# Expert weight loads and splits placed by the program on ACT, POOL and DVE

## The chip, the core and the metric

The kernel runs on one core of one Trainium2 chip. The metric is the device time of one launch in microseconds, the median of several runs. Five engines work side by side, each through its own instruction list in order: TensorE (PE: matmuls, with PEld for the loading of their stationary operands), VectorE (DVE), ScalarE (ACT), GpSimd (POOL), and SyncE (SP), which here only issues DMA transfers.

## What is computed

Sparse causal attention, then a dense layer pair, then eight experts that each take exactly 288 of 2304 tokens.

```python
attn_out = _attn_ref(q, k, v)                # 4 x 8 heads, 576 tokens, 64 wide; two masks
x = attn_out.transpose(0, 2, 1, 3).reshape(2304, 512)
h = x @ w_in                                 # 512 -> 2048
x = np.maximum(0.01 * h, h) @ w_out          # 2048 -> 512
logits = x @ w_gate                          # 8 experts
# pairs (token, expert) in falling order of logit; a token goes to the first expert
# in this order that has room left (288 places each) -> assigned
for e in range(8):
    mask = assigned == e
    h = np.maximum(x[mask] @ w1[e], 0.0)     # 512 -> 1024
    out[mask] = h @ w2[e]                    # 1024 -> 512
```

## The kernel before

**Numbers in two halves.** Every large matrix product is made of three: each fp32 operand is split into a high part in the matmul's own format and the rest, and high x high, high x low and low x high are added up. For a weight tile the high part is a copy on ACT (`hi`, `whi`) and the low part a subtraction on POOL or DVE (`lo`, `wlo`), which must wait for that copy.

**Dense layers.** Tokens go in six blocks of 384. Blocks 0 to 2 pass both layers at once. For blocks 3 to 5 the first layer is run with its results kept (`gd`) or sent to DRAM (`g3d`), and the second layer follows as `second(4)`, `second(5)`, `second(3)`: each has 16 steps `f`, and a step splits one row of `WO` (`split`: `hi` on ACT, `lo` on POOL, two buffers each) and runs nine matmuls of 512 columns (L944 to L946: `hi`, `lo`, `hi` again with the low half of the activations). The last step copies the block out and stores it in `x2d`, from which `gather` later takes an expert's rows.

**Routing.** The greedy assignment is a search on DVE and PE (`search`, `route`, `tokens`, all through one helper at L683): for each of eight rounds k, five threshold counts. A count is: DVE compares (`G`, about 1.4 us for a tile), PE sums (`cnt`, 18 small matmuls), DVE makes a `flag`, PE sums it to `tot`. After the fifth comes a chain of some dozen small DVE operations to the expert's number `ei` and to a pair `tot`, PE makes prefix sums (`po`, L775), DVE makes places, PE gathers them (`pi`, L813), and DVE writes the row numbers `idx`. `pace` takes so many steps of this per step of the dense layer or of an expert, so that the search of later rounds runs under the matmuls of `second` and of the first experts.

**Experts.** `expert(k)` has 32 steps of six matmuls. 16 make `h` (`g3`, L878 to L880; after each two steps ACT writes `hh` and DVE `hl`), 16 make the output (`g4`, L901 to L903), which is turned back (`back`, ACT copies it to `o`) and scattered to DRAM by three indirect DMAs that POOL issues (`put`, L917). The turning of the last quarter and the scatter are put off to the second pair of steps of the next expert. `gather(k + 1)` runs in the last ten steps: POOL issues three indirect DMAs (`xg`, L851), PE turns the rows (`pet`), ACT and DVE split them (`exh`, `exl`).

**Expert weights.** `weights(k)` is a generator over eight pieces of 512 KB, n = 0 to 3 of `w1` and 4 to 7 of `w2`. For each it issues the load on SP into one of three `raw` buffers, copies `whi` on ACT, and subtracts `wlo`: on DVE for n = 1, 5 and 7, on POOL for the rest. `wx` for expert 0 is stepped four times in `second(3)` and finished after `gather(0)`; for expert k + 1 it is made at step 3 of expert k (`values_load` reads the expert's number into SP) and stepped at the even steps from 6 on. The `w2` halves have five buffers, in a pool (`POOLB`) that can only be opened when `second(3)` has ended.

**What sets the order.** The program text gives each instruction a priority and its dependencies; a scheduler then puts each engine's list together and may move an instruction forward as soon as its own model of time has its inputs ready. The search goes through `Soon`, which raises its priority by 2000.

Of the kernel before, what the change touches and what calls it, by code (L numbers as in the profile page):

```python
# [7 lines left out]
F32 = mybir.dt.float32  # L8
F32R = mybir.dt.float32r
# [3 lines left out]
AF = mybir.ActivationFunctionType  # L13
# [5 lines left out]
DM, FF = 512, 2048  # L19
# [7 lines left out]
def body(ctx, tc, q, k, v, w_in, w_out, w_gate, w1, w2, out):  # L27
    nc = tc.nc
# [7 lines left out]
    xa = ctx.enter_context(tc.tile_pool(name="xa", bufs=1, reuse_waits="tile"))  # L36
# [260 lines left out]
    WI = [xa.tile([128, 2, 512], F32, name="WI", tag=f"WI{f}") for f in range(8)]  # L297
    WI = [WI[f // 2][:, f % 2] for f in range(16)]
# [288 lines left out]
    for n in range(64, 96):  # L587
        blk, f = divmod(n, 16)
# [11 lines left out]
        if f % 4 == 0:  # L600
            x = "hl"[f // 4 % 2]
# [53 lines left out]
    m, kh, e1, rem, s, sel, oh = (state(n) for n in (18, 18, 18, 18, 18, 18, 8))  # L655
# [29 lines left out]

    soon = Soon()

    def search():

        soon.tensor_reduce(m, L, axis=AX.X, op=OP.max)  # L690
# [131 lines left out]
    def ind(ap):  # L822
        return bass.IndirectOffsetOnAxis(ap=ap, axis=0)

    def weights(k):
        e = nc.values_load(EXP[k][0:1, 0:1], engines=[mybir.EngineType.SP], min_val=0, max_val=7)
        W[k] = []
        for n in range(8):
            raw = POOLA[0].tile([128, 1024], F32, name="raw", tag="raw", bufs=3)
            if n < 4:  # L830
                nc.sync.dma_start(raw, w1[bass.ds(e, 1), 128 * n:128 * n + 128, :].rearrange("e p m -> (e p) m"))
            else:
                nc.sync.dma_start(raw.rearrange("p (j m) -> p j m", j=2),
                                  w2[bass.ds(e, 1), 256 * (n - 4):256 * (n - 4) + 256, :].rearrange(
                                      "e (j p) m -> p (e j) m", j=2))
            if n < 4 and k % 2:
                hi, lo = (xa.tile([128, 1024], F32R, name="w" + x, tag=f"WI{n + y}") for x, y in (("hi", 0), ("lo", 4)))
            else:
                pool, tag, bufs = (POOLB[0], "w2", 5) if n >= 4 else (POOLA[0], "w1", 4)
                hi = pool.tile([128, 1024], F32R, name="whi", tag=tag + "h", bufs=bufs)  # L840
                lo = pool.tile([128, 1024], F32R, name="wlo", tag=tag + "l", bufs=bufs)
            nc.scalar.activation(hi, raw, AF.Copy)  # L842
            (nc.vector if n in (1, 5, 7) else nc.gpsimd).tensor_sub(lo, raw, hi.bitcast(F32))  # L843
            W[k].append((hi, lo))
            yield

    def gather(k):
        xg = xa.tile([96, 3, DM], F32, name="xg", tag=("xh2", "xl2")[k % 2])
# [20 lines left out]
    def expert(k):  # L869
# [4 lines left out]
        for j in range(8):  # L874
# [9 lines left out]
                left_.pop()()  # L884
            nc.scalar.activation(hh[:, j], p, AF.Relu)  # L885
            nc.vector.scalar_tensor_tensor(hl[:, j], p, 0.0, hh[:, j].bitcast(F32), op0=OP.max, op1=OP.subtract)  # L886
        o = e2.tile([96, 3, DM], F32, name="o", tag="o", bufs=2)

        def back(c, ot):
            pt = bank([96, 3, 128], "pot", "m")  # L890
# [71 lines left out]
    def need(k):  # L962
        while ROUTED[0] <= k:
            next(R, None)
# [16 lines left out]
        if f > 2 and f % 2:  # L981
            fetch(f // 2)
    need(0)
    wx = weights(0)
    for f, _ in enumerate(second(3)):
        pace(0.87)
        if f < 8:
            fetch(f + 8)
        if f % 4 == 1:
            next(wx)  # L990
    right.close()
    POOLB[0] = ctx.enter_context(tc.tile_pool(name="pbx", bufs=1, reuse_waits="tile", side="right"))
    for _ in gather(0):
        pass
    for _ in wx:
        pass
    for k in range(8):
        nxt = iter(())
        for n, _ in enumerate(expert(k)):
            pace(0.45)  # L1000
            if n == 3 and k < 7:
                need(k + 1)
                wx = weights(k + 1)
            if n >= 6 and n % 2 == 0:
                next(wx, None)
            if n == 22 and k < 7:
                nxt = gather(k + 1)
                next(nxt)
            if n >= 22:
                next(nxt, None)  # L1010
        for x in (wx, nxt):
            for _ in x:
                pass


# [28 lines left out]
```

## Time and profile before

| | us |
|---|---|
| median of 3 runs (911.5 to 913.36) | 913.01 |
| the profiled execution, its own time | 920.74 |
| its span, first to last instruction | 919.0 |
| PE busy in it | 860.8 |
| DVE busy | 567.6 |
| POOL busy | 473.1 |
| ACT busy | 442.7 |

The profile follows one execution; times in it are counted from its first instruction. A matmul's end is modelled, and matmuls overlap, so the distance from start to start tells more than the busy time. PEclk is TensorE's granted clock as a share of 2.4 GHz; 0.5 is its other level, 1.2 GHz. The dense layers' last three blocks run from 505 to 634 us, the experts from 643 to 906.

### The profile page before, as it was taken

How to read it: one execution, taken by the hardware profiler on the slowest of the kernel's cores; microseconds unless marked ns; L12 is line 12 of the kernel's file. 1: busy time of each engine (PE TensorE's matmuls, PEld its weight loads, DVE VectorE, ACT ScalarE, POOL GpSimd, SP SyncE). 2: the span in 40 equal slices, each digit the busy share in tenths (PEclk: the TensorE clock that was granted, in tenths of full speed). 3: DMA queues.
4: the chain of work that ended last, by engine and by line, in shares of the span. 5: the costliest groups of instructions: out<-in, count | busy, mean ns of one | idle time of the engine just before them, and what ended most of it. 6: DMA issues, size and time to landing. Idle time of an engine off the chain costs nothing.

```text
span 919.0 us, 17020 instructions
## 1 busy us (share of the span) xinstructions
PE 860.8 (94%) x6272; PEld 723.8 (79%) x6272; DVE 567.6 (62%) x1537; ACT 442.7 (48%) x1098; POOL 473.1 (51%) x394
## 2 busy tenths in 40 slices
PE   8789999799999999999999998996998899999994
PEld 5667766677777777788988776775998899899994
DVE  5778798865546455566545463455677888784330
ACT  4787757464545445544554232222453443535531
POOL 2645655564555465554554455554643625736621
PEclk8899999999999999999999997998999999999998
DMA  7487555420112000142000033342644534626700
GB/s 178 121 191 171 136 147 143 130 61 14 37 35 78 14 14 1 52 157 102 1 1 18 1 104 128 118 139 72 201 153 130 190 114 143 192 96 210 209 27 26
DMA packets 95411, 93.18 MB, mean 101 GB/s; under 512 B 66144, under 2 KB 74336, under 8 KB 95328
## 3 DMA queue, kind: packets, MB, share of 16 engines
q1 hardware_dynamic: 87648, 65.88, 25.2%
q0 software_dynamic: 7680, 26.22, 9.3%
q8 instruction: 49, 0.80, 0.4%
q14 instruction: 34, 0.28, 0.1%
HBM read 76.35 MB, written 15.73 MB: 100 GB/s over the span
## 4 chain that ended last, share of the span: by engine, by line
PE 66%; DVE 9%; DMA 7%; issue 6%; POOL 5%; ACT 4%; SPq 1%; POOLq 0%; ACTq 0%; DVEq 0%
PE p L421 4%; PE q L944 4%; PE p L423 4%; PE p L374 3%; PE p L422 3%; PE q L945 3%; PE q L946 3%; PE p L398 3%; PE g L901 3%; PE g L902 3%; DMA raw<-in_moe_w_dram 3%; PE g L903 3%; PE p L376 3%; PE p L375 3%; PE p L400 3%
## 5 line engine op out<-in xcount | busy, mean ns | idle before, releaser
L353 POOL TENSOR_TENSOR lo<-WI,hi 128x512 fp32r<-128x512 f32 x96 | 127.3, 1326 | 99.2 <-DVE hi L352 58.2
L353 POOL TENSOR_TENSOR lo<-WO,hi 128x512 fp32r<-128x512 f32 x96 | 124.9, 1302 | 97.4 <-ACT hi L350 97.3
L843 POOL TENSOR_TENSOR wlo<-raw,whi 128x1024 fp32r<-128x1024 f32 x40 | 98.1, 2465 | 71.5 <-ACT whi L842 66.7
L350 ACT ACTIVATE hi<-WO 128x512 fp32r<-128x512 f32 x96 | 60.5, 630 | 109.4 <-PE q L946 66.5
L842 ACT ACTIVATE whi<-raw 128x1024 fp32r<-128x1024 f32 x64 | 65.9, 1055 | 45.1 <-DMA raw<-in_moe_w_dram 42.3
L374 PE MATMUL p<-xh,hi 128*128 128x384 f32 x192 | 75.6, 394 | 5.4 <-DVE g L383 5.4
L878 PE MATMUL g<-exh,whi 128*128 128x288 f32 x256 | 79.4, 311 | 0.2 <-DVE hl L886 0.2
L901 PE MATMUL g<-hh,whi 128*128 128x288 f32 x256 | 78.8, 308 | 0.6 <-ACT hh L885 0.6
L879 PE MATMUL g<-exl,whi 128*128 128x288 f32 x256 | 78.1, 306 | 0.0
L880 PE MATMUL g<-exh,wlo 128*128 128x288 f32 x256 | 77.6, 303 | 0.0
L902 PE MATMUL g<-hl,whi 128*128 128x288 f32 x256 | 76.3, 298 | 0.1
L903 PE MATMUL g<-hh,wlo 128*128 128x288 f32 x256 | 76.0, 297 | 0.0
L160 ACT ACTIVATE sc<-sc,mx 96x128 f32<-96x128 f32 (+2 forms) x176 | 67.6, 387 | 16.1 <-DVE mx L158 16.1
L376 PE MATMUL p<-xh,lo 128*128 128x384 f32 x192 | 66.0, 344 | 1.5 <-POOL lo L353 1.5
L421 PE MATMUL p<-xh,hi 128*128 128x384 f32 x192 | 66.4, 346 | 0.0
L375 PE MATMUL p<-xl,hi 128*128 128x384 f32 x192 | 65.8, 342 | 0.6 <-DVE xl L235 0.6
L423 PE MATMUL p<-xh,lo 128*128 128x384 f32 x192 | 64.7, 337 | 0.7 <-POOL lo L353 0.7
L398 PE MATMUL p<-hi,gh 128*128 128x512 f32 x144 | 64.1, 445 | 0.7 <-ACT gh L384 0.7
L422 PE MATMUL p<-xl,hi 128*128 128x384 f32 x192 | 64.4, 335 | 0.0
L182 POOL TENSOR_TENSOR sc<-sc,mx 96x384 f32<-96x384 f32 (+2 forms) x64 | 51.5, 822 | 21.3 <-DVE mx L180 14.0
L400 PE MATMUL p<-hi,gl 128*128 128x512 f32 x144 | 56.9, 395 | 0.0
L843 DVE TENSOR_TENSOR wlo<-raw,whi 128x1024 fp32r<-128x1024 f32 x24 | 47.4, 1976 | 15.1 <-ACT whi L842 15.0
(209 smaller groups left out, 2313.0 us busy)
## 6 DMA issues: line engine op xcount, KB each, us to landing
raw<-in_moe_w_dram SPq DMA_DIRECT2D x64, 512.0 KB
wraw<-in_moe_w_in_dram POOLq DMA_DIRECT2D x16, 512.0 KB, 4.6
wraw<-in_moe_w_out_dram POOLq DMA_DIRECT2D x16, 512.0 KB, 3.9
g<-g3d SPq DMA_DIRECT2D x16, 384.0 KB
rawq<-in_q_dram SPq DMA_DIRECT2D x32, 144.0 KB
rawk<-in_k_dram SPq DMA_DIRECT2D x32, 144.0 KB
x2d<-x SPq DMA_DIRECT2D x18, 256.0 KB
g3d<-gh SPq DMA_DIRECT2D x16, 192.0 KB
```

The source lines that it names most:

```text
L353: nc.gpsimd.tensor_sub(lo, src, hi.bitcast(F32))
L374: nc.tensor.matmul(p1, wh[:, cs], xh[:, c], start=(c == 0), stop=False)
L375: nc.tensor.matmul(p1, wh[:, cs], xl[:, c], start=False, stop=False)
L376: nc.tensor.matmul(p1, wl[:, cs], xh[:, c], start=False, stop=(c == 3))
L398: nc.tensor.matmul(p2[t], gh[:, s], oh, start=(f == 0), stop=False)
L421: nc.tensor.matmul(p1, wh[:, cs], xh[:, c], start=(c == 0), stop=False)
L422: nc.tensor.matmul(p1, wh[:, cs], xl[:, c], start=False, stop=False)
L423: nc.tensor.matmul(p1, wl[:, cs], xh[:, c], start=False, stop=(c == 3))
L843: (nc.vector if n in (1, 5, 7) else nc.gpsimd).tensor_sub(lo, raw, hi.bitcast(F32))
L901: nc.tensor.matmul(p, wh, hh[:, j], start=(j == 0), stop=False)
L902: nc.tensor.matmul(p, wh, hl[:, j], start=False, stop=False)
L903: nc.tensor.matmul(p, wl, hh[:, j], start=False, stop=(j == 7))
```

## The change

`weights` is split into `load(k, n)`, which issues one transfer, and `halves(k, n)`, which makes `whi` and `wlo` of it. Both operations of `halves` are passed to `pin`, which orders each behind the instruction that the program text has just ahead of it on the same engine; what comes later in the text may still be moved ahead of it. There are four `raw` buffers. Of the eight subtractions n = 5 and 7 stay on DVE, n = 1 goes to POOL. The output tile `o` has one buffer in place of two. Expert 0's first four loads are issued ahead of `second(3)`, whose steps 3, 6, 9 and 12 make their halves and issue the next loads; the table `CH` gives the steps of an expert (1, 4, 7 for its own pieces 5 to 7, then 10, 14, 18, 22, 26 for pieces 0 to 4 of the next) and at each of them the next expert's next load.

```diff
+    def pin(x):
+        tc.keep_in_program_order(x[0] if isinstance(x, tuple) else x)
...
-    def weights(k):
-        e = nc.values_load(EXP[k][0:1, 0:1], engines=[mybir.EngineType.SP], min_val=0, max_val=7)
-        W[k] = []
-        for n in range(8):
-            raw = POOLA[0].tile([128, 1024], F32, name="raw", tag="raw", bufs=3)
...
-            nc.scalar.activation(hi, raw, AF.Copy)
-            (nc.vector if n in (1, 5, 7) else nc.gpsimd).tensor_sub(lo, raw, hi.bitcast(F32))
-            W[k].append((hi, lo))
-            yield
+    def load(k, n):
+
+        if n == 0:
+            W[k] = []
+            REG[k % 2] = nc.values_load(EXP[k][0:1, 0:1], engines=[mybir.EngineType.SP], min_val=0, max_val=7)
+        e = REG[k % 2]
+        raw = POOLA[0].tile([128, 1024], F32, name="raw", tag="raw", bufs=4)
...
+        RAWE[k, n] = raw
...
+    def halves(k, n):
+        raw = RAWE.pop((k, n))
...
+        pin(nc.scalar.activation(hi, raw, AF.Copy))
+        pin((nc.vector if n in (5, 7) else nc.gpsimd).tensor_sub(lo, raw, hi.bitcast(F32)))
+        W[k].append((hi, lo))
...
-        o = e2.tile([96, 3, DM], F32, name="o", tag="o", bufs=2)
+        o = e2.tile([96, 3, DM], F32, name="o", tag="o")
...
-    wx = weights(0)
+    for n in range(4):
+        load(0, n)
     for f, _ in enumerate(second(3)):
         pace(0.87)
         if f < 8:
             fetch(f + 8)
-        if f % 4 == 1:
-            next(wx)
+        if f in (3, 6, 9, 12):
+            halves(0, f // 3 - 1)
+            if f < 12:
+                load(0, 3 + f // 3)
...
-    for _ in wx:
-        pass
+    halves(0, 4)
+    load(0, 7)
+    CH = {n: i for i, n in enumerate((1, 4, 7, 10, 14, 18, 22, 26))}
     for k in range(8):
         nxt = iter(())
         for n, _ in enumerate(expert(k)):
             pace(0.45)
-            if n == 3 and k < 7:
-                need(k + 1)
-                wx = weights(k + 1)
-            if n >= 6 and n % 2 == 0:
-                next(wx, None)
+            if n in CH:
+                c = CH[n]
+                if c < 3:
+                    halves(k, 5 + c)
+                elif k < 7:
+                    halves(k + 1, c - 3)
+                if k < 7:
+                    need(k + 1)
+                    load(k + 1, c)
```

The list of POOL from the start of `second(4)` to the first expert, before (lines L353 are `lo` of `WO`, L843 `wlo`, L851 the gathers' DMAs):

```order
L353 TENSOR_TENSOR lo<-WO,hi 128x512 x17
L843 TENSOR_TENSOR wlo<-raw,whi 128x1024
L353 TENSOR_TENSOR lo<-WO,hi 128x512 x3
L843 TENSOR_TENSOR wlo<-raw,whi 128x1024 x2
L353 TENSOR_TENSOR lo<-WO,hi 128x512 x26
L851 DMA xg<-x2d,idx 96x512 x6
```

and in the changed kernel (L855 is `wlo`, L862 the gathers):

```order
L353 TENSOR_TENSOR lo<-WO,hi 128x512 x34
L855 TENSOR_TENSOR wlo<-raw,whi 128x1024
L353 TENSOR_TENSOR lo<-WO,hi 128x512 x3
L855 TENSOR_TENSOR wlo<-raw,whi 128x1024
L353 TENSOR_TENSOR lo<-WO,hi 128x512 x3
L855 TENSOR_TENSOR wlo<-raw,whi 128x1024
L353 TENSOR_TENSOR lo<-WO,hi 128x512 x3
L855 TENSOR_TENSOR wlo<-raw,whi 128x1024
L353 TENSOR_TENSOR lo<-WO,hi 128x512 x3
L862 DMA xg<-x2d,idx 96x512 x6
```

Three `wlo` stood in `second(5)`, two of them in a row; now four stand singly in `second(3)`, from its fourth `lo` on.

The list of DVE in expert 1, where the fifth count of a search round ends, before (L886 is `hl`, L683 the search, `flag` the fifth count's):

```order
L683 TENSOR_SCALAR flag,f_7732<-cnt 64x8
L886 SCALAR_TENSOR_TENSOR hl<-g_7706,hh 128x288
L683 TENSOR_REDUCE n<-tot 128x1
L683 TENSOR_SCALAR o_7753<-tot,n 128x8
L683 TENSOR_TENSOR st<-o_7753,st 128x8
L683 TENSOR_REDUCE e_7756<-st 128x1
L843 TENSOR_TENSOR wlo<-raw,whi 128x1024
L683 TENSOR_SCALAR st<-st,e_7756 128x8
```

and in the changed kernel, from the end of the same chain (L897 is `hl`, the CAST writes the `tot` that PE's `po` reads, `s` is the first to read `po`):

```order
L897 SCALAR_TENSOR_TENSOR hl<-g_7797,hh 128x288
L683 CAST ei<-ev 128x1
L683 SCALAR_TENSOR_TENSOR st<-st,ab 128x36
L683 CAST tot<-st 128x2
L855 TENSOR_TENSOR wlo<-raw,whi 128x1024
L683 SCALAR_TENSOR_TENSOR s_7822<-st,po,ab 128x18
L897 SCALAR_TENSOR_TENSOR hl<-g_7812,hh 128x288
```

The subtraction left the middle of the chain and stands behind the `tot` that PE waits for, but ahead of the last three `hl`.

The list of DVE in expert 3 of the changed kernel, from the third count to the fifth:

```order
L683 SCALAR_TENSOR_TENSOR G<-th_5738,zero_5748,st 128x1152
L855 TENSOR_TENSOR wlo<-raw,whi 128x1024
L683 TENSOR_SCALAR flag,f_8786<-cnt 64x8
L897 SCALAR_TENSOR_TENSOR hl<-g_8723,hh 128x288
L683 SCALAR_TENSOR_TENSOR G<-th_5734,tot,st 128x1152 x2
L897 SCALAR_TENSOR_TENSOR hl<-g_8760,hh 128x288
L897 SCALAR_TENSOR_TENSOR hl<-g_8804,hh 128x288
L683 TENSOR_SCALAR flag,f_8858<-cnt 128x8
L855 TENSOR_TENSOR wlo<-raw,whi 128x1024
L683 SCALAR_TENSOR_TENSOR G<-th_5736,tot,st 128x1152
```

Both subtractions (n = 5, then n = 7) stand inside the search, the second between a `flag` and the next count's `G`.

## Rows read from the trace of the kernel before

**Rows 1.** The page's busy times: us, share of the span, instructions.

```profile
PE 860.8 (94%) x6272; PEld 723.8 (79%) x6272; DVE 567.6 (62%) x1537; ACT 442.7 (48%) x1098; POOL 473.1 (51%) x394
```

**Rows 2.** Windows: second(5), second(3), experts; busy us PE PEld DVE ACT POOL; clock; DMA.

```profile
542.00:592.60 50.60, 45.63 (x263) 34.25 (x263) 23.33 (x53) 16.09 (x24) 28.98 (x20) 0.90 0.42 136
592.60:634.00 41.40, 39.87 (x254) 29.99 (x253) 23.14 (x65) 12.32 (x21) 20.14 (x16) 1.00 0.38 120
...
643.00:906.00 263.00, 253.19 (x2213) 245.16 (x2212) 172.68 (x415) 114.83 (x213) 129.95 (x77) 0.98 0.46 146
```

**Rows 3.** Waits of PE in second(5): for whom, us in total, times, longest.

```profile
PE q L945 <- POOL lo L353: 5.0, 3, 2.9
```

**Rows 4.** Waits of PE in experts 1 to 7 (676 to 906 us).

```profile
PE tot L732 <- DVE flag L683: 3.8, 5, 1.7
PE po L775 <- DVE tot L683: 3.5, 2, 3.4
PE cnt L725 <- DVE G L683: 1.6, 2, 0.8
PE g L901 <- ACT hh L885: 0.6, 1, 0.6
```

**Rows 5.** Timeline of POOL in second(5): start, us, instruction, idle before and its end.

```profile
549.16 2.39 POOL L843 TENSOR_TENSOR wlo<-raw,whi 128x1024 fp32r<-128x1024 f32 x1 [0.95 <-DMA x2d<-x]
558.50 5.70 POOL L843 TENSOR_TENSOR wlo<-raw,whi 128x1024 fp32r<-128x1024 f32 x2
```

**Rows 6.** Timeline of PE: waits in second(5), expert 1 and expert 2.

```profile
552.84 0.61 PE L945 MATMUL q<-lo,g5h 128*128 128x512 f32 x1 [1.80 <-POOL lo L353]
...
692.98 0.16 PE L775 MATMUL po<-tot,tri 128*128 128x2 bf16 x1 [3.36 <-DVE tot L683]
729.30 0.16 PE L732 MATMUL tot<-f,units 64*128 64x1 bf16 x1 [1.74 <-DVE flag L683]
```

**Rows 7.** Windows after the four longest waits; clock is the third number from the end.

```profile
553.00:557.00 4.00, 4.00 (x23) 3.10 (x24) 0.23 (x1) 0.90 (x2) 1.02 (x1) 0.57 0.28 115
566.00:574.00 8.00, 8.00 (x37) 6.08 (x36) 0.17 (x2) 1.13 (x2) 1.94 (x2) 0.57 0.36 131
693.00:697.00 4.00, 4.00 (x20) 4.00 (x20) 2.12 (x9) 1.47 (x2) 2.79 (x2) 0.57 0.81 309
730.00:734.00 4.00, 4.00 (x21) 4.00 (x20) 2.20 (x12) 1.32 (x2) 2.38 (x1) 0.57 0.64 243
```

**Rows 8.** Timeline of POOL in second(3): `lo` of steps 4 and 7.

```profile
601.13 1.29 POOL L353 TENSOR_TENSOR lo<-WO,hi 128x512 fp32r<-128x512 f32 x1 [0.95 <-ACT hi L350]
...
607.50 1.29 POOL L353 TENSOR_TENSOR lo<-WO,hi 128x512 fp32r<-128x512 f32 x1 [0.79 <-ACT hi L350]
```

**Rows 9.** Timeline of PE in second(3): the first matmuls that read those two `lo`.

```profile
602.49 0.49 PE L945 MATMUL q<-lo,g 128*128 128x512 f32 x1
...
609.75 0.39 PE L945 MATMUL q<-lo,g 128*128 128x512 f32 x1
```

**Rows 10.** All uses of tile raw: duration ns min/median/max; then who waited.

```profile
L843 POOL TENSOR_TENSOR wlo<-raw,whi x40: 2348/2397/3384, 549.2 to 879.1; 128x1024 fp32r<-128x1024 f32 x40
L843 DVE TENSOR_TENSOR wlo<-raw,whi x24: 1209/1226/5885, 557.4 to 880.0; 128x1024 fp32r<-128x1024 f32 x24
...
  ACT whi L842: 42.3, 25
```

**Rows 11.** Timeline of POOL in expert 1.

```profile
681.11 0.94 POOL L917 DMA_INDIRECT out_dram<-o,idx  x1 [3.68 <-DMA raw<-in_moe_w_dram]
...
684.51 4.76 POOL L843 TENSOR_TENSOR wlo<-raw,whi 128x1024 fp32r<-128x1024 f32 x2
```

**Rows 12.** Timeline of DVE: subtractions in experts 1, 2 and 3.

```profile
684.47 5.88 DVE L843 TENSOR_TENSOR wlo<-raw,whi 128x1024 fp32r<-128x1024 f32 x1
725.03 4.13 DVE L843 TENSOR_TENSOR wlo<-raw,whi 128x1024 fp32r<-128x1024 f32 x1
749.04 1.22 DVE L843 TENSOR_TENSOR wlo<-raw,whi 128x1024 fp32r<-128x1024 f32 x1
```

More of the change, by code (lines that the diff above doesn't have):

```diff
@@ L823, in ind @@
         return bass.IndirectOffsetOnAxis(ap=ap, axis=0)
-    def weights(k):
-        e = nc.values_load(EXP[k][0:1, 0:1], engines=[mybir.EngineType.SP], min_val=0, max_val=7)
-        W[k] = []
-        for n in range(8):
-            raw = POOLA[0].tile([128, 1024], F32, name="raw", tag="raw", bufs=3)
[L830 to L841, printed above, removed]
-            nc.scalar.activation(hi, raw, AF.Copy)
-            (nc.vector if n in (1, 5, 7) else nc.gpsimd).tensor_sub(lo, raw, hi.bitcast(F32))
-            W[k].append((hi, lo))
-            yield
@@ new lines, in load @@
+    def load(k, n):
[4 more added lines that the diff above has]
+        raw = POOLA[0].tile([128, 1024], F32, name="raw", tag="raw", bufs=4)
+        if n < 4:
+            nc.sync.dma_start(raw, w1[bass.ds(e, 1), 128 * n:128 * n + 128, :].rearrange("e p m -> (e p) m"))
+        else:
+            nc.sync.dma_start(raw.rearrange("p (j m) -> p j m", j=2),
+                              w2[bass.ds(e, 1), 256 * (n - 4):256 * (n - 4) + 256, :].rearrange(
+                                  "e (j p) m -> p (e j) m", j=2))
+        RAWE[k, n] = raw
@@ new lines, in body @@
+    REG, RAWE = [None, None], {}
+    def halves(k, n):
+        raw = RAWE.pop((k, n))
+        if n < 4 and k % 2:
+            hi, lo = (xa.tile([128, 1024], F32R, name="w" + x, tag=f"WI{n + y}") for x, y in (("hi", 0), ("lo", 4)))
+        else:
+            pool, tag, bufs = (POOLB[0], "w2", 5) if n >= 4 else (POOLA[0], "w1", 4)
+            hi = pool.tile([128, 1024], F32R, name="whi", tag=tag + "h", bufs=bufs)
+            lo = pool.tile([128, 1024], F32R, name="wlo", tag=tag + "l", bufs=bufs)
+        pin(nc.scalar.activation(hi, raw, AF.Copy))
+        pin((nc.vector if n in (5, 7) else nc.gpsimd).tensor_sub(lo, raw, hi.bitcast(F32)))
+        W[k].append((hi, lo))
@@ L1010, in body @@
                 next(nxt, None)
-        for x in (wx, nxt):
-            for _ in x:
-                pass
+        for _ in nxt:
+            pass
 _INS = ['q', 'k', 'v', 'moe_w_in', 'moe_w_out', 'moe2_w_gate', 'moe2_w1', 'moe2_w2']
```

## The prediction

> **What bounds the kernel now.** The page's busy times come first [rows 1]: PE is busy 860.8 of 919.0 us, so only what PE waits for, or does slowly, can be won. The windows by stage say where that is [rows 2]. The experts take 263 us with PE busy 253.19, and `second(5)` takes 50.6 us where the like-sized `second(3)` takes 41.4. POOL's busy time there is 28.98 against 20.14 us.
>
> The waits of PE name the causes. In `second(5)` PE waits 5.0 us in three pieces, all for POOL's `lo` [rows 3]. POOL's timeline shows what stood ahead of those `lo`: one `wlo` of 2.39 us at 549.16, and two in a row, 5.70 us, at 558.50 [rows 5]. PE's wait of 1.80 us, until 552.84 [rows 6], ends behind the first, the longest, 2.9, behind the pair. In experts 1 to 7 PE waits 3.8 us for `flag`, 3.5 for `tot`, 1.6 for `G`, all of them search steps on DVE, and 0.6 for ACT: 9.5 us in ten pieces [rows 4].
>
> A wait has a second price. After these two waits in `second(5)`, and after two in the experts (3.36 us at 692.98, 1.74 us at 729.30 [rows 6]), the granted clock falls to its lower level, 1.2 GHz, and comes back only after a while: four stretches of 4, 8, 4 and 4 us have a mean of 0.57 [rows 7]. What is lost is 0.43 of each: 1.7, 3.4, 1.7 and 1.7 us. Shorter waits (0.8 us and less, the rest of rows 4) left no such mark.
>
> So what the weight splits cost PE is 5.0 + 1.7 + 3.4 = 10.1 us in `second(5)`, and 9.5 + 1.7 + 1.7 = 12.9 us in the experts.
>
> Why DVE is late in the experts is told by its own subtractions [rows 12]. The same instruction takes 1.22 us at 749.04, 4.13 at 725.03 and 5.88 at 684.47; the median of 24 is 1226 ns [rows 10]. The 5.88 us is POOL's doing: POOL ran two subtractions from 684.51 to 689.27 [rows 11], and DVE's ended 1.08 us after them. Whichever of the two engines comes second stands still, and the search steps behind DVE's subtraction stand with it.
>
> The Trainium skill, page "SBUF — State Buffer", section "Who interferes with whom", has this as a rule: a VectorE instruction with two SBUF inputs and a GpSimd instruction that reads SBUF exclude each other for a whole instruction, and the first to issue goes first. The rule alone would let DVE stand for at most one POOL subtraction; the row at 684.47 has it stand for two in a row, and the row decides. By the rule the residue worked out below would be capped at the value that I take for it, 6.0 us; by the row it can be 15.
>
> **The change, part by part.**
>
> *`second(5)`.* The order of POOL shows no `wlo` there any more. All 10.1 us go. What is late next is PE itself: 50.6 - 10.1 = 40.5 us is about what `second(3)`, without a `wlo`, takes with its copy out, 41.4 [rows 2].
>
> *`second(3)`.* Four `wlo` now stand there, each alone, behind the `lo` of steps 3, 6, 9 and 12. POOL's `lo` of step 4 starts at 601.13 after 0.95 us of idling, so that of step 3 ended at 600.18 [rows 8]. With a `wlo` of 2.40 us between, the next starts at 602.58, 1.45 us later, and ends at 603.87; PE reads it at 602.49 and had 0.07 us to spare [rows 8, 9]. Cost: 1.4 us. At step 6 `lo` ends at 606.71 (607.50 less 0.79), a `wlo` would at 609.11, and the next `lo` is 1.61 us late; its slack is 609.75 - 608.79 = 0.96. Cost: 0.65. At steps 9 and 12 the search's matmuls stretch the steps, the same sum leaves nothing. Together 2.1 us. A wait of 1.4 lies between the 0.8 that left the clock alone and the 1.74 that did not; I take no fall, and 1.7 us as the upper end. The four copies `whi` run while ACT waits for PE. The loads are issued in `second(5)`, and the three that stand between the fetches of `g3d` on SP hold only fetches that are read eight steps later: nothing.
>
> *Third subtraction from DVE to POOL.* DVE loses 8 x 1.23 = 9.8 us of work and a third of its meetings with POOL; POOL gains 8 x 2.40 = 19.2 us. In the experts POOL is busy 129.95 of 263 us and PE never waits for it [rows 2, 4]. Cost on the path: nothing directly.
>
> *Pinned places.* In experts 1 to 4 of the changed kernel the `wlo` of n = 5 comes about 2 to 6 us into the expert, when POOL has no subtraction; I cost it at 0. The one of n = 7 is the trouble. ACT makes its `whi` behind the third `hh`, some 7 us in, and the search has DVE there at some 10 us (both by the matmuls that stand ahead in PE's list, at the same 0.11 us and the DVE steps between). POOL meanwhile has the three scatter DMAs, which in expert 1 ran from 681.11 until the subtractions began at 684.51 [rows 11], some 5 us after that expert's start; only then the `wlo` of n = 6, and close behind it the first of the next expert. So POOL's subtractions lie from about 9 us in to 12 or 14: right where DVE comes with n = 7. The bounds of one such meeting: nothing (1.22 us in all at 749.04 [rows 12]), and 5.88 - 1.22 = 4.66 us. I take one POOL subtraction, 2.40 us, as the row nearest to it is 725.03 with 4.13 - 1.22 = 2.9. Cover: matmuls that PE has queued ahead of what it needs from DVE (in expert 1, 24 between `po` and the next stage, at 253.19 / 2213 = 0.11 us each [rows 2] some 2.7 us), of which I count 0.9 us, an estimate, since the search's own chain uses the rest. That leaves 1.5 us in each of four experts, 6.0 us. I add 0.4 us for short waits and one fall of the clock, 1.7: 8.1 us in place of 12.9. Gain 4.8.
>
> *Fourth buffer, earlier loads.* ACT's `whi` waited 42.3 us for loads [rows 10], the cause of the 0.6 us that PE waits for `hh` in expert 6 [rows 4]; a load now goes out about three chunk steps, some 9 us, ahead of its use. The 0.6 is in the 12.9.
>
> *One `o` buffer, the earlier register load.* The first copy into `o` comes after 20 of an expert's 32 steps, the scatter of the expert before is issued some 8 us into it [rows 11]: nothing.
>
> **The sum.** 10.1 - 2.1 + 4.8 = 12.8 us. On the profiled execution 920.74, span 919.0 and 1.7 around it, becomes 907.9. The median of the runs, 913.01, lies 7.7 us below the profiled one; I take the same microseconds off it: 900.2.
>
> **The rivals.**
>
> *Clean order.* If the subtraction of n = 7 meets POOL in no expert, only the 0.4 us of short waits and a fall in none stay: 10.1 - 2.1 + 12.5 = 20.5, 892.5. For it: before, DVE ran a subtraction undisturbed even with a search in hand (749.04 [rows 12]), and the median of all 24 is 1226 ns. Against it: the scatter holds POOL's n = 6 back in every expert.
>
> *Starved, in four experts.* Each meeting costs the full 4.66 less 0.9, and the clock falls each time: 4 x (3.8 + 1.7) = 22 us against 12.9. Gain 10.1 - 2.1 - 9.1 = -1.1: 914.1, no measurable change (0.2%, some 1.8 us, is about what a measurement of this kernel can tell). If the pinned order only moves the waits of the experts and all 12.9 us come back, 8.0 are left and the time is 905.0, inside the forecast's band.
>
> *Slower.* DVE starves in all five experts with a search on DVE's list ahead of it (0 to 4), PE stands with it (no cover, since in experts 1 and 2 the next thing on its list is the search's own matmul), and the clock falls each time: 5 x (4.66 + 1.7) = 31.8 against 12.9. Then -8.0 + 18.9 = +10.9: 923.9. It decides from (12.9 + 8.0) / 5 = 4.2 us an expert on. For it: six subtractions an expert on POOL, and a scatter that bunches them. Against it: expert 1's place, where `tot` is already cast.
>
> **How the numbers follow.** Forecast, with one to three bad meetings (895 to 908): 0.50. Clean (888 to 895): 0.27. No change: 0.10. Slower: 0.08. Between the forecast and no change (908 to 911): 0.05. Faster by over 0.2% is 0.50 + 0.27 + 0.05 = 0.82, the same 0.10, slower 0.08. The range for 8 in 10: at the low end part of the clean case, 889; at the high end 909, which leaves out the two last cases and a little of the one before.
>
> **What would show it.** Right: `second(5)` at some 40 us, clock 1.00 throughout; `second(3)` at 43 to 44 with one wait of about 1.4 us for `lo` right behind the first `wlo`; DVE's `wlo` of n = 5 at 1.2 us, those of n = 7 over 2 us in experts 1 to 4, with a PE wait for `tot`, `G` or `hl` behind them; ACT's wait for loads near nothing. Wrong: a PE wait for a `wlo` or `whi` itself, falls of the clock in `second(3)`, or n = 7 at 1.2 us throughout, which would be the clean case.

## The result and the profile after

The changed kernel takes 901.96 us (median; 898.73 to 904.97), the kernel before beside it on the same chip 911.09. The ratio is 0.9884, interval 0.9856 to 0.9912: by it 10.6 us faster, between 8.0 and 13.1; the two medians lie 9.1 us apart. The forecast was 900.2 us and 12.8 us of gain.

The profiled execution of the changed kernel has a span of 900.1 us. Busy times of its page, as [rows 1]:

```profile
PE 851.0 (95%) x6272; PEld 715.9 (80%) x6272; DVE 542.8 (60%) x1529; ACT 441.8 (49%) x1098; POOL 491.9 (55%) x402
```

PE is busy 9.8 us less, with the same 6272 matmuls. By windows of 2 us from the second layers on, the lower clock cost 13.6 us before and 6.8 now; that is 6.8 of it. The windows of `second(5)`, `second(3)` and the experts, columns as in [rows 2]:

```profile
539.50:580.40 40.90, 40.63 (x262) 30.94 (x262) 20.20 (x52) 12.28 (x20) 21.13 (x17) 1.00 0.39 129
580.40:624.00 43.60, 40.46 (x251) 29.99 (x250) 23.41 (x65) 15.03 (x23) 29.38 (x20) 1.00 0.50 161
633.00:887.00 254.00, 250.25 (x2213) 242.97 (x2212) 152.13 (x410) 117.81 (x216) 145.71 (x84) 0.99 0.48 148
```

`second(5)` went from 50.6 to 40.9 us with its clock at 1.00 throughout, `second(3)` from 41.4 to 43.6, the experts from 263 to 254. Their clock of 0.99 is the end of a fall that all these kernels have in the gather just ahead. What PE still waits for in the first two windows and in the experts, as [rows 3, 4]:

```profile
PE q L956 <- POOL lo L353: 1.9, 3, 1.2
...
PE cnt L729 <- DVE G L683: 2.1, 3, 0.9
PE tot L736 <- DVE flag L683: 1.1, 1, 1.1
PE po L779 <- DVE tot L683: 0.3, 1, 0.3
PE g L912 <- DVE exl L875: 0.2, 1, 0.2
```

Of the 5.0 us for `lo` in `second(5)` only 0.27 us are left, a short wait at 544.19 that the kernel before has too (0.25). `second(3)` has 1.6 us instead, which makes the 1.9 of the first line. The experts' 9.5 us became 3.7. Where `second(3)` waits can be seen on POOL, then on PE (timelines; columns as in [rows 8, 9]):

```profile
588.02 2.39 POOL L855 TENSOR_TENSOR wlo<-raw,whi 128x1024 fp32r<-128x1024 f32 x1
590.38 2.52 POOL L353 TENSOR_TENSOR lo<-WO,hi 128x512 fp32r<-128x512 f32 x2
...
591.69 0.51 PE L956 MATMUL q<-lo,g 128*128 128x512 f32 x1 [1.17 <-POOL lo L353]
599.58 0.50 PE L956 MATMUL q<-lo,g 128*128 128x512 f32 x1 [0.45 <-POOL lo L353]
```

The first `wlo` pushes the next two `lo` together, and PE waits 1.17 us for the first of them. Behind the second `wlo` it waits 0.45, behind the other two not at all. And on all uses of `raw`, as [rows 10], DVE's subtractions and what ACT waited for:

```profile
L855 DVE TENSOR_TENSOR wlo<-raw,whi x16: 1215/1222/2468, 637.2 to 868.4; 128x1024 fp32r<-128x1024 f32 x16
...
  ACT whi L854: 2.9, 2
```

ACT's wait for loads fell from 42.3 us to 2.9, and DVE's worst subtraction from 5.88 to 2.47 us.

### The profile page after: what moved, and what is told of

Its sections match the earlier page's. It is cut to its first block, busy times and chain, and to the rows that moved or that the text cites. A ratio compares the mean times of both kernels' runs of the same rounds, so it can differ in the third digit from the quotient of the medians.

```text
span 900.1 us, 17006 instructions
## 1 busy us (share of the span) xinstructions
PE 851.0 (95%) x6272; PEld 715.9 (80%) x6272; DVE 542.8 (60%) x1529; ACT 441.8 (49%) x1098; POOL 491.9 (55%) x402
## 5 line engine op out<-in xcount | busy, mean ns | idle before, releaser
L353 POOL TENSOR_TENSOR lo<-WI,hi 128x512 fp32r<-128x512 f32 x96 | 127.6, 1329 | 98.7 <-DVE hi L352 58.1
L353 POOL TENSOR_TENSOR lo<-WO,hi 128x512 fp32r<-128x512 f32 x96 | 125.8, 1312 | 90.2 <-ACT hi L350 90.1
L855 POOL TENSOR_TENSOR wlo<-raw,whi 128x1024 fp32r<-128x1024 f32 x48 | 116.6, 2443 | 28.4 <-ACT whi L854 23.7
L160 ACT ACTIVATE sc<-sc,mx 96x128 f32<-96x128 f32 (+2 forms) x176 | 67.6, 387 | 17.3 <-DVE mx L158 17.2
L928 POOL DMA_INDIRECT out_dram<-o,idx x24 | 24.2, 1009 | 73.8 <-ACT o L904 62.0
```

What stands on the lines that cost most here:

```text
L160: nc.scalar.activation(s[:nq, h, i, :nk], s[:nq, h, i, :nk], AF.Exp, bias=mx[:nq, 0, h, i:i + 1], scale=-1.0, accum_out=mx[:nq, 1, h, i:i ...
L353: nc.gpsimd.tensor_sub(lo, src, hi.bitcast(F32))
L855: pin((nc.vector if n in (5, 7) else nc.gpsimd).tensor_sub(lo, raw, hi.bitcast(F32)))
```

## The experiments

Two stretches of each profile are compared, by the distance from start to start: the **second layers**, from the first matmul of `second(4)` to the first of the experts, and the **experts**, from there to their last matmul. What no edit touches, the first 500 us, is left out. "Waits" are PE's in the experts, pieces over 0.2 us; "loads" is ACT's wait for loads over the whole execution.

| kernel | pinned | steps | raw | subtractions on DVE | second layers | experts | waits | loads | ratio to before |
|---|---|---|---|---|---|---|---|---|---|
| before | no | old | 3 | 1, 5, 7 | 137.6 | 263.1 | 9.5 | 42.3 | 1 |
| before, second profile | no | old | 3 | 1, 5, 7 | 137.6 | 265.7 | 10.4 | 39.2 | 0.9987 |
| pin first expert | 4 pieces | old | 3 | 1, 5, 7 | 130.8 | 264.1 | 11.4 | 39.5 | 0.9949 |
| pin all | yes | old | 3 | 1, 5, 7 | 130.9 | 264.6 | 9.6 | 26.8 | 0.9969 |
| pin all, four raw | yes | old | 4 | 1, 5, 7 | 130.8 | 254.7 | 4.3 | 6.0 | 0.9883 |
| changed, three raw | yes | new | 3 | 5, 7 | 130.0 | 257.9 | 4.7 | 16.4 | 0.9920 |
| changed | yes | new | 4 | 5, 7 | 130.1 | 254.1 | 3.7 | 2.9 | 0.9884 |
| changed, second profile | yes | new | 4 | 5, 7 | 130.0 | 254.9 | 3.6 | 2.4 | 0.9850 |
| n = 1 on DVE | yes | new | 4 | 1, 5, 7 | 130.7 | 254.0 | 3.7 | 3.4 | 0.9834 |
| no pin | no | new | 4 | 5, 7 | 133.0 | 278.1 | 20.5 | 60.6 | 1.0182 |
| n = 6 on DVE | yes | new | 4 | 5, 6 | 130.0 | 252.8 | 2.5 | 0.6 | 0.9882 |
| only n = 5 on DVE | yes | new | 4 | 5 | 130.0 | 250.5 | 1.7 | 0.9 | 0.9819 |
| later steps | yes | later | 4 | 5, 7 | 128.7 | 254.5 | 3.8 | 2.9 | 0.9860 |
| later steps, n = 6 | yes | later | 4 | 5, 6 | 128.7 | 250.5 | 2.0 | 0 | 0.9799 |

**How well the stretches repeat.** The kernel before, unchanged, a second time:

> The kernel before, profiled once more. Its first profiled execution took 920.74 us where the runs without a profile had 911 as median; the changed kernel's took 901.9 where its runs had 902. Theory A (the waits behind POOL and DVE have a price that changes from execution to execution, through the moments at which loads land): second(5) and the experts come out some us shorter or longer than 50.6 and 263 in this look, with waits of PE between 5 and 15 us in the experts. Theory B (the profile itself adds the same to it each time): span 917 to 920 again, the same waits within 0.3 us.

Ratio 0.9987 (0.9959 to 1.0015). The second layers took 137.6 us both times, with nearly the same waits for `lo` (1.80 and 2.93 us, then 1.91 and 2.89). The experts took 2.6 us more: behind one DVE subtraction of 6.4 us that the first profile does not have, PE waited 2.1 us for `hl`. The untouched stretch ahead varied by more, 505.4 and then 501.0 us. So the second layers repeat as theory B has it, and the experts vary as theory A has it. That the profile itself adds time is not shown: this profiled execution, 918.96 us, lies within the twelve of its kernel, 911.87 to 922.40.

The changed kernel, unchanged, a second time:

> The changed kernel a second time, beside the next three on one chip. In its first profile the stretch from the first matmul of second(4) to the first expert's took 130.1 us and the experts 254.1. Theory A (the program's fixed order sets these stages): both repeat within 0.5 us, the ratio lies inside the first interval, 0.9856 to 0.9912. Theory B (part of the 9.0 us won in the experts was one good execution): the experts take 256 us or more.

Ratio 0.985 (0.9812 to 0.9889), 903.71 us. Second layers 130.0, experts 254.9: theory A for the second layers and nearly so for the experts. The ratio misses the first interval, 0.9856 to 0.9912, from below, though the two intervals overlap. The experts' 0.8 us more come with one place in expert 4, shown further down.

**The second layers: are the moved subtractions all of it?** Only expert 0's first four pieces pinned, all else as before:

> The kernel before, with only the copies and subtractions of expert 0's first four pieces kept in their place in the text (steps 1, 5, 9 and 13 of second(3)); nothing changed in the experts. Theory A (two places each give a part): second(5) falls from 50.6 us to about 40.5, the clock stays at 1.00 in it, second(3) gets 1 to 3 us longer; the experts stay at 260 to 263; the time is 5 to 8 us below before. Theory B (the gain comes from the experts alone): the time is within 2 us of before, the 10 us won in second(5) being lost again in second(3).

```diff
...
-            nc.scalar.activation(hi, raw, AF.Copy)
-            (nc.vector if n in (1, 5, 7) else nc.gpsimd).tensor_sub(lo, raw, hi.bitcast(F32))
+            x = nc.scalar.activation(hi, raw, AF.Copy)
+            y = (nc.vector if n in (1, 5, 7) else nc.gpsimd).tensor_sub(lo, raw, hi.bitcast(F32))
+            if k == 0 and n < 4:
+                pin(x)
+                pin(y)
```

Ratio 0.9949 (0.9922 to 0.9976). `second(5)`, between the copies out of two blocks, fell from 49.3 to 39.6 us, the changed kernel's value, and the second layers to 130.8: 6.8 of the 7.5 us that the whole change gains there. Theory A. The experts, at 264.1, lie between the two profiles of before.

The same four pieces at later steps of the changed kernel's `second(3)`:

> The changed kernel with expert 0's first four halves made in steps 6, 9, 11 and 13 of second(3) in place of 3, 6, 9 and 12, each with its load behind it. Theory A (what a subtraction there costs is 2.40 us less POOL's idle time and the slack of the lo behind it): only the one at step 6 costs, 0.4 to 0.7 us; PE's waits for lo fall from 1.6 to about 0.6 us and second(3) from 41.0 to about 39.8; experts unchanged at 254. Theory B (each subtraction costs about the same wherever it stands, or the loads come too late for the experts): second(3) within 0.4 us of 41.0, or the first expert longer by over 1 us.

```diff
-        if f in (3, 6, 9, 12):
-            halves(0, f // 3 - 1)
-            if f < 12:
-                load(0, 3 + f // 3)
+        if f in (6, 9, 11, 13):
+            n = (6, 9, 11, 13).index(f)
+            halves(0, n)
+            if n < 3:
+                load(0, 4 + n)
```

Ratio 0.986 (0.9833 to 0.9888), 900.16 us. PE's waits for `lo` fell from 1.9 to 0.7 us and the second layers to 128.7. Theory A by the stretches: the wait behind the first `wlo` was the price of the step that it stands at. By time the run can't be told from the changed kernel (0.9884).

**The experts: order, table or buffer?** Everything pinned (the edit of the run with four pieces, without its condition), but the old steps and three buffers:

> The kernel before, with all copies and subtractions kept in their place in the text, but the old steps, three buffers for raw and the subtractions of n = 1, 5 and 7 on DVE. Theory A (the place of a subtraction in DVE's list decides): second(5) as in the run above, and the experts at 256 to 259 us, part of the way to the changed kernel's 254; the time 8 to 11 us below before. Theory B (pinning helps second(5) alone; in the experts the table of steps, the fourth buffer and n = 1 on POOL do it): the experts at 262 to 264, the time that of the run above.

```diff
...
+            if True:
+                pin(x)
+                pin(y)
```

Ratio 0.9969 (0.9937 to 1.0002): no change that can be measured against before, slower than with only four pieces pinned if anything. The experts take 264.6 us. But the waits are other ones. PE's in the experts, then ACT, PE and the clock at the longest, and PE and the clock at the next (waits; timelines; windows):

```profile
PE g L908 <- ACT hh L892: 4.7, 2, 2.4
PE po L779 <- DVE tot L683: 1.9, 3, 1.3
...
823.47 1.06 ACT L846 ACTIVATE whi<-raw 128x1024 fp32r<-128x1024 f32 x1 [3.63 <-DMA raw<-in_moe_w_dram]
824.43 0.39 ACT L892 ACTIVATE hh<-g 128x288 fp32r<-128x288 f32 x1
826.90 1.06 ACT L846 ACTIVATE whi<-raw 128x1024 fp32r<-128x1024 f32 x1 [2.07 <-DMA raw<-in_moe_w_dram]
827.86 0.39 ACT L892 ACTIVATE hh<-g 128x288 fp32r<-128x288 f32 x1
...
828.31 0.40 PE L908 MATMUL g<-hh,whi 128*128 128x288 f32 x1 [2.40 <-ACT hh L892]
...
828.00:834.00 6.00, 5.60 (x30) 5.39 (x31) 0.49 (x2) 1.14 (x4) 4.63 (x2) 0.72 0.52 164
...
861.05 0.40 PE L908 MATMUL g<-hh,whi 128*128 128x288 f32 x1 [2.26 <-ACT hh L892]
...
861.00:867.00 6.00, 5.86 (x46) 5.65 (x46) 1.66 (x4) 2.19 (x6) 2.17 (x1) 1.00 0.48 173
```

The search's waits fell from before's 8.9 us (`flag`, `tot`, `G` in [rows 4]) to 3.5 (`po` 1.9, `cnt` 1.1, `pi` 0.5). In their place ACT stands twice for a load with `hh` queued behind the copy, PE waits 2.40 us for that `hh`, and the clock falls: 0.72 over 6 us, 1.7 us lost. A second wait of this kind, 2.26 us at 861.05, left the clock at 1.00. The only other fall in the experts comes with a wait of 1.53 us for `hl` at 655.35; there it is DVE's `idx` ahead of that `hl` which took 2.33 us beside POOL's subtractions (0.15 us in the run without a pin, at 698.23). Theory B as to the time. The fixed order did take the subtractions out of the search's way, and these waits, 4.7 us of them for `hh` behind late loads, took it all back.

The fourth buffer alone added to that (and one `o` buffer, to make room):

> The kernel before with every half pinned, four raw buffers and one o buffer, but its own steps (n = 1 on DVE). With three buffers these steps gave experts of 264.6 us, and the new table of steps gave 257.9 with three buffers and 254.1 with four. Theory A (the table is what counts, the fourth buffer adds the 3.8 us that it was worth there): 260 to 261.5. Theory B (the fourth buffer is of use only where the loads are issued earlier; the old steps issue load and copy together, so that the copy waits as before): 263.5 to 265.5. Theory C (four buffers alone mend the experts): 255 or less.

```diff
-            raw = POOLA[0].tile([128, 1024], F32, name="raw", tag="raw", bufs=3)
+            raw = POOLA[0].tile([128, 1024], F32, name="raw", tag="raw", bufs=4)
...
-        o = e2.tile([96, 3, DM], F32, name="o", tag="o", bufs=2)
+        o = e2.tile([96, 3, DM], F32, name="o", tag="o")
```

Ratio 0.9883 (0.9845 to 0.992), 904.76 us. Theory C: 254.7 us, 9.9 below three buffers, without the new table. The intervals of the two ratios lie apart. The waits for `hh` are gone, and ACT's for loads are down from 26.8 to 6.0 us. This run says a second thing. Uses of `raw`; DVE and POOL (timelines); PE's waits in the experts:

```profile
L847 DVE TENSOR_TENSOR wlo<-raw,whi x24: 1208/1650/7815, 600.9 to 862.6; 128x1024 fp32r<-128x1024 f32 x24
...
  ACT whi L846: 6.0, 6
...
812.05 6.34 DVE L847 TENSOR_TENSOR wlo<-raw,whi 128x1024 fp32r<-128x1024 f32 x1
840.85 7.82 DVE L847 TENSOR_TENSOR wlo<-raw,whi 128x1024 fp32r<-128x1024 f32 x1 [0.49 <-ACT whi L846]
848.59 1.54 DVE L893 SCALAR_TENSOR_TENSOR hl<-g,hh 128x288 fp32r<-128x288 f32 x4
...
812.55 4.75 POOL L847 TENSOR_TENSOR wlo<-raw,whi 128x1024 fp32r<-128x1024 f32 x2
840.44 10.47 POOL L847 TENSOR_TENSOR wlo<-raw,whi 128x1024 fp32r<-128x1024 f32 x4
...
PE g L909 <- DVE hl L893: 1.5, 1, 1.5
PE cnt L729 <- DVE G L683: 1.1, 2, 0.7
PE tot L736 <- DVE flag L683: 1.0, 1, 1.0
PE po L779 <- DVE tot L683: 0.6, 2, 0.4
```

DVE stood behind POOL longer than in any other kernel here: over all its subtractions 24.4 us above 1.22 us each, against 18.2 in before and 4.3 in the changed kernel. PE waited 4.3 us in all; in experts 0 to 4 DVE stood 9.8 us and PE waited 2.4. The 6.34 us at 812.05 cost it nothing, the 7.82 us with four `hl` behind them 1.5. So what DVE loses this way says little of what PE waits.

The changed kernel with three buffers again:

> The changed kernel with three buffers for raw in place of four; every engine's list is the same. Theory A (the experts gain because the table lets loads go out early enough, and that needs the fourth buffer; with pinning and three buffers alone they stayed at 264.6 us): ACT's copies wait for loads again, by 15 us and more in total, PE waits for hh or hl in experts 0, 5 or 6, the experts take 257 to 262 us. Theory B (the table's places alone do it): the experts stay within 1 us of 254.1.

```diff
-        raw = POOLA[0].tile([128, 1024], F32, name="raw", tag="raw", bufs=4)
+        raw = POOLA[0].tile([128, 1024], F32, name="raw", tag="raw", bufs=3)
```

Ratio 0.992 (0.9892 to 0.9948), 905.25 us. Experts 257.9, 3.8 us more, with a wait of 1.25 us for `hh` at 851.53 and one clock fall (behind a wait for `flag`). Theory A by the stretches; the interval of this ratio overlaps that of the changed kernel. With the run before, the square is full: with three buffers the new table is worth 264.6 - 257.9 = 6.7 us, with four 0.6. The move of n = 1 to POOL stands in both differences, and in the first the single `o` buffer too; with four buffers n = 1 made no difference (next group), with three it was not tried. The loads that ACT waits for, 26.8 us at the old steps, 16.4 at the new and 6.0 with the fourth buffer, fit one reading: earlier loads and one more buffer are two ways to a load that is there when the copy comes.

The changed kernel without pinning:

> The changed kernel without the pinning: same steps, four buffers, two subtractions on DVE, but the scheduler may move copies and subtractions ahead. Theory A (pinning is what clears second(5), the table and the buffer what helps the experts): the three subtractions stand in second(5) again, which takes 48 to 50 us, with falls of the clock; the experts stay at 254 to 257; the time is 6 to 9 us above the changed kernel. Theory B (without the pinning the experts lose too, as DVE's subtractions stand in the search again): the experts at 258 to 263, the time near that of the kernel before.

```diff
-        pin(nc.scalar.activation(hi, raw, AF.Copy))
-        pin((nc.vector if n in (5, 7) else nc.gpsimd).tensor_sub(lo, raw, hi.bitcast(F32)))
+        nc.scalar.activation(hi, raw, AF.Copy)
+        (nc.vector if n in (5, 7) else nc.gpsimd).tensor_sub(lo, raw, hi.bitcast(F32))
```

Ratio 1.0182 (1.0149 to 1.0216), 931.43 us: slower than before, by more than either theory had, and nearer to B. ACT and PE at the longest wait (timelines):

```profile
846.81 1.06 ACT L854 ACTIVATE whi<-raw 128x1024 fp32r<-128x1024 f32 x1 [9.23 <-DMA raw<-in_moe_w_dram]
847.77 0.39 ACT L896 ACTIVATE hh<-g 128x288 fp32r<-128x288 f32 x1
...
848.22 0.61 PE L912 MATMUL g<-hh,whi 128*128 128x288 f32 x1 [7.24 <-ACT hh L896]
```

Left free, the copies move ahead on ACT's list, to places where their loads are not there: ACT waits 60.6 us for loads, in one place 9.23, and PE 7.24 for the `hh` behind. Not all of it is loads, though: 3.38 us of PE's waits, for a `flag` at 790.59, stand behind a DVE subtraction of 5.66 us. Theory A had the place of `second(5)` right and its price too high: all four `wlo` stand there again, but it took 44.7 us between the copies out in place of 48 to 50, with one clock fall. The table and the buffer are worth something only behind the pin. Four buffers in the kernel before without a pin were not tried.

**Which subtractions on DVE?** n = 1 back to DVE:

> The changed kernel with the subtraction of n = 1 back on DVE (three of eight). Theory A (each DVE subtraction in an expert with a search can meet one of POOL's and then holds the search): DVE's subtractions of n = 1 take 2 us and more in at least three of experts 1 to 5, PE's waits on DVE in the experts grow by 2 to 5 us, the time is 904 to 907. Theory B (POOL's load counts as much as DVE's): POOL's bunches get shorter, DVE's n = 7 meets fewer, the time is 900 to 903, as the changed kernel.

```diff
-        pin((nc.vector if n in (5, 7) else nc.gpsimd).tensor_sub(lo, raw, hi.bitcast(F32)))
+        pin((nc.vector if n in (1, 5, 7) else nc.gpsimd).tensor_sub(lo, raw, hi.bitcast(F32)))
```

Ratio 0.9834 (0.979 to 0.9878), 900.6 us, experts 254.0, second layers 130.7. Theory B as to the time: the third subtraction on DVE or on POOL is the same. Its reason did not come, as DVE met POOL for longer, 9.3 us in place of 4.3.

n = 6 on DVE, n = 7 on POOL:

> The changed kernel with n = 6 on DVE and n = 7 on POOL. DVE's second subtraction of an expert then comes some 2 us earlier, while POOL issues the scatter and has no subtraction yet. Theory A (the stretched n = 7, 1.4 to 2.5 us in experts 1 to 4, is a meeting with POOL's subtraction and costs PE what stands behind it): DVE's subtractions take 1.2 us in experts 1 to 5 and the waits of PE in experts 3 and 4 (3.2 us in the profile) fall under 1.5 us; experts at 251 to 253. Theory B (they are the price of DVE's amount of work in the search): the waits stay within 0.7 us of 3.7, experts at 253.5 to 255.

```diff
-        pin((nc.vector if n in (5, 7) else nc.gpsimd).tensor_sub(lo, raw, hi.bitcast(F32)))
+        pin((nc.vector if n in (5, 6) else nc.gpsimd).tensor_sub(lo, raw, hi.bitcast(F32)))
```

Ratio 0.9882 (0.9857 to 0.9907), 902.61 us. One meeting is left, in expert 3, 3.83 us long with a PE wait of 1.68 us behind; all others are at 1.2. Experts 252.8, 1.3 us less by the profile; by time it can't be told from the changed kernel. Mostly theory A.

Only n = 5 left on DVE (`n == 5` in the same line):

> The changed kernel with n = 7 on POOL too, so that only n = 5 is left on DVE: POOL has 7 of 8 subtractions. Theory A (the subtraction of n = 7 standing behind POOL's is what is left of PE's 3.7 us of waits in the experts): no subtraction of DVE over 1.3 us, waits of some 1 us, experts 251.5 to 252.5. Theory B (DVE's lateness is the search's own chain): waits of 3 to 4 us and 254 as before. Theory C (three subtractions in a row on POOL behind the scatter come too late): a wait of PE or PEld for POOL's wlo, experts over 255.

Uses of `raw`, and PE's waits in the experts:

```profile
L855 DVE TENSOR_TENSOR wlo<-raw,whi x8: 1216/1218/1228, 633.5 to 854.7; 128x1024 fp32r<-128x1024 f32 x8
...
PE g L912 <- DVE exl L875: 1.4, 1, 1.4
PE cnt L729 <- DVE G L683: 0.5, 2, 0.3
```

Ratio 0.9819 (0.9778 to 0.986), 898.74 us. No subtraction is held up, the search's waits are down to 0.5 us, and the experts take 250.5. It is theory A, a little better than it said, with one new wait of 1.4 us for `exl` that it did not have; 1.9 of the 3.6 us against the changed kernel lie in the first expert (32.4 and 34.3 us), where the clock was back sooner after the gather, so 1.7 are the subtraction's. By time it can't be told from the changed kernel on the same chip (0.985). POOL, with seven of eight subtractions, is never waited for by PE.

**The two edits together.** Later steps and n = 5, 6 on DVE:

> The two edits that shortened a stage put together: expert 0's halves at steps 6, 9, 11 and 13, and n = 5 and 6 on DVE in place of 5 and 7. Alone, the first took 1.4 us from the second layers (128.7 in place of 130.1), the other 1.3 us from the experts (252.8 in place of 254.1). Theory A (the stages are apart, the gains add up): 128.7 and 252.8, 2.7 us or 0.3% below the changed kernel. Theory B (the copy of expert 0's fourth piece now lies too near its use, so that what was won comes back in the first expert): 128.7 and 254 or more.

Ratio 0.9799 (0.9758 to 0.9841), 899.06 us, where the changed kernel on the same chip took 903.71 (0.985). Both intervals touch, so time alone does not part them; the stretches do: 128.7 + 250.5 = 379.2 us against 130.0 + 254.9 = 384.9. Theory A, with 2.3 us more than it said; 1.7 of them are the first expert again (32.6 us, the clock back at 637.5 in a stretch from 635.2, where the changed kernel's came back at 638.0 in one from 633.0). The best ratio measured here is this one, though its interval overlaps that of n = 5 alone.

## Why the prediction came out

**`second(5)`, 10.1 us.** Right: 9.7 us, with 0.27 us of waits and no clock fall left, and pinning four pieces is enough for it. What is late next was PE itself, as forecast: 40.9 us against the 40.5 worked out.

**`second(3)`, 2.1 us.** Right: 43.6 - 41.4 = 2.2. The two waits are where they were put, 1.17 us behind the first `wlo` (1.4 forecast) and 0.45 behind the second (0.65), nothing behind the others. That makes 1.6 us of waits for 2.05 forecast; where the other 0.6 of the 2.2 us lie is not shown, so the sum came out nearer than its parts. The choice to take no clock fall held, 1.00 throughout, but the rows that it leaned on could not give it: in other runs waits of up to 2.26 us left the clock alone and behind one of 0.86 it fell (last section).

**n = 1 to POOL, nothing.** Right. The single `o` buffer and the earlier register load were not tried apart; PE waits for nothing of theirs.

**The residue in the experts, 8.1 us.** This is the mis-sized term: 3.7 us of waits and no clock fall in the first profile. The place of the meetings was right. DVE's n = 5 ran in 1.22 us everywhere, its n = 7 behind POOL's n = 6 in experts 1 to 4, and in expert 0 too (1.94 us, with no wait behind it). Timelines of DVE, and of POOL in expert 2:

```profile
678.76 1.40 DVE L855 TENSOR_TENSOR wlo<-raw,whi 128x1024 fp32r<-128x1024 f32 x1
...
710.87 2.42 DVE L855 TENSOR_TENSOR wlo<-raw,whi 128x1024 fp32r<-128x1024 f32 x1
...
744.08 2.47 DVE L855 TENSOR_TENSOR wlo<-raw,whi 128x1024 fp32r<-128x1024 f32 x1
...
779.47 2.16 DVE L855 TENSOR_TENSOR wlo<-raw,whi 128x1024 fp32r<-128x1024 f32 x1
...
709.79 2.41 POOL L855 TENSOR_TENSOR wlo<-raw,whi 128x1024 fp32r<-128x1024 f32 x1
```

A meeting was priced at one whole POOL subtraction, 2.40 us. Over 1.22 us these four are 0.18, 1.20, 1.25 and 0.94. POOL had been at it for 1.0 to 1.3 us when DVE came in experts 2 to 4, and in expert 1 DVE came in between POOL's two. The waits just behind them are 0.30 (`po`, expert 2), 0.63 and 0.90 us (`G`, experts 3 and 4), 1.8 us in place of 6.0. The other 1.9 us of PE's waits stand behind no held subtraction (`flag`, one `G`, `exl`); 0.4 were forecast. No clock fall: 1.7 us less. Together 4.4 us, and the experts did gain 9.0 where 4.8 was forecast.

A full price is possible, though. In the second profile of the same kernel the meeting of expert 4 was one (timelines of DVE, POOL and PE; a window):

```profile
778.65 4.03 DVE L855 TENSOR_TENSOR wlo<-raw,whi 128x1024 fp32r<-128x1024 f32 x1
...
778.24 0.92 POOL L928 DMA_INDIRECT out_dram<-o,idx  x1 [0.31 <-issue]
779.19 2.40 POOL L855 TENSOR_TENSOR wlo<-raw,whi 128x1024 fp32r<-128x1024 f32 x1
781.77 3.13 POOL L855 TENSOR_TENSOR wlo<-raw,whi 128x1024 fp32r<-128x1024 f32 x1 [0.18 <-ACT whi L854]
...
784.07 0.38 PE L729 MATMUL cnt<-C,G 128*128 128x8 bf16 x9 [2.10 <-DVE G L683]
...
784.00:790.00 6.00, 5.93 (x47) 5.72 (x48) 4.13 (x8) 1.73 (x4) 2.91 (x2) 0.72 0.62 214
```

DVE lost 2.8 us, PE waited 2.10 for the `G` behind, and the clock fell behind it (0.72 over 6 us, 1.7 us lost): 3.8 us where one meeting with a fall was put at 1.5 + 1.7. Expert 2's meeting was longer there too, 3.28 us, with a wait of 0.35. The bounds were right; that all four would lie in their middle was not, and where in the bounds a meeting falls changes from one execution to the next.

**The fourth buffer, 0.6 us.** Wrong, and this is the step where the reasoning failed and not only a size. ACT's 42.3 us of waiting for loads were read by what they cost PE in the kernel before, 0.6 us. But pinning fixes the copies in front of `hh`, so that a late load becomes a late `hh`. With three buffers the pin took 8.9 - 3.5 = 5.4 us of waits from the search and its two clock falls, and gave as much back in waits for `hh` and `hl` (0.8 us before, 6.2 with the pin, 4.7 of them for `hh`) and two falls of their own (264.6 us). The fourth buffer is worth 9.9 us at the old steps, 3.8 at the new ones. The total came out because the table and the buffer arrived in one change; of the pin alone the same reasoning would have forecast a gain in the experts that does not exist. The forecast did name the case that the pinned order only moves the experts' waits, at 905.0 us, but no rival had a late load as the new wait.

**From the profiled execution to the median.** The two stretches gained 7.5 + 9.0 = 16.5 us in the first pair of profiles and 18.4 in the second; the timings say 10.6 (8.0 to 13.1) and 13.7 (10.2 to 17.2). In the second pair the untouched stretch ahead took 3.8 us longer in the changed kernel (504.8 and 501.0), which leaves 14.6; in the first it was 2.4 shorter. The two pairs are not alike in other ways: the first profile of before, 920.74 us, lies above all six of its timed runs (907.90 to 913.36), the changed kernel's, 901.87, in the middle of its own, and the second pair was taken on two chips. Whether that stretch is longer in the median too isn't settled. The forecast's 12.8 against 10.6 is within this.

**The rivals.** The clean order (892.5 us) did not come, but its condition can be had: with only n = 5 on DVE no subtraction is held, and the experts take 250.5 us. Its 20.5 us of gain would be 7.5 + 12.6 = 20.1 by these stretches, and its ratio is worth 16.6 us (12.8 to 20.3). Starved and slower, a full meeting with a clock fall in four or five experts, did not come in any run of these steps; one long meeting with a fall did, in expert 4 of the second profile. That a held DVE alone does not make them is shown by the old steps with four buffers, 9.8 us of standing in experts 0 to 4 and 2.4 us of PE's waits there.

## What to carry to other kernels

Fixing the place of an operation that depends on a transfer gains only if the transfer is there in time: look at what that engine waits for in the version where the operation could still move, and count what stands behind it on its list as exposed to the whole of that wait. A wait that costs nothing today because the order gives way is not the price of that wait once the order is fixed. And price a collision by the waits behind it, not by the time that the held engine loses.

## What the runs showed of the hardware

**DVE behind POOL.** A two-input subtraction on DVE can stand through several of POOL's: 6.34 us behind two, 7.82 us behind three (840.44 plus three of 2.4 us is 847.6, and DVE ended at 848.67). The Trainium skill, page "SBUF — State Buffer", section "Who interferes with whom", says that the two exclude each other and that the first to issue goes first. The exclusion agrees with these rows. The order does not, as far as the start of a record tells the issue: at 778.65 in the second profile of the changed kernel DVE's record starts 0.54 us ahead of POOL's first subtraction, which still ran its undisturbed 2.40 us. POOL's scatter was being issued when DVE started, there and at 812.05 (old steps, four buffers); whether that is what held DVE was not tried apart. It can't be all: at 840.85 in the latter run no scatter was being issued, and POOL's second and third subtraction, at 842.81 and 845.18, went ahead of a DVE that had come before them. Nor is it always POOL that goes on: at 678.76 in the changed kernel DVE came in between two of POOL's and was done in 1.40 us.

**The clock after a wait.** There is no one length of wait from which it falls. After PE's waits of 1.70 (in the run with later steps), 2.10 and 2.40 us it fell; after 1.17, 1.25, 1.68 (with n = 6 on DVE) and 2.26 us (all pinned, 861.05) it did not. In the second profile of before it fell behind a wait of 0.86 us at 790.53 (0.72 over the 6 us from 790). And of two waits for the same `flag` in expert 4, 1.11 us at 779.23 in the changed kernel left it at full speed, and 1.06 us with three buffers did not (timeline and window of that run):

```profile
779.86 0.16 PE L736 MATMUL tot<-f,units 64*128 64x1 bf16 x1 [1.06 <-DVE flag L683]
...
779.00:784.00 5.00, 4.14 (x20) 4.05 (x19) 4.36 (x6) 1.35 (x2) 3.23 (x2) 0.66 0.47 144
```

**The stretch that nothing touches.** The time to the first matmul of `second(4)` lay between 499.3 and 506.9 us over these profiles, in no order with the edits. That is 0.8% of the span, more than several of the effects above, which is why they were read by stretches.
